# Reordering the products, the background work and the buffer slots of an attention and two-GEMM kernel on one core

## The chip, the cores and the metric

The kernel runs on one NeuronCore of a Trainium2 chip. The metric is device microseconds of one execution, the median of several runs. The profiler names the engines: PE (TensorE, the matmul engine, with its weight loads shown apart as PEld), DVE (VectorE), ACT (ScalarE), POOL (GpSimd) and SP (SyncE, which here only issues DMAs). Each engine works through its own instructions in program order and meets the others at semaphores.

## The reference: what is computed

```python
# q, k, v: (4, 12, 448, 64)
scores = np.where(upper_triangle, -1e9, (q @ k.transpose(0, 1, 3, 2)) / 8)
attn = softmax(scores)
x = (attn @ v).transpose(0, 2, 1, 3).reshape(1792, 768)
h = x @ w_in                                       # w_in (768, 2048)
g = np.maximum(h, 0) + alpha * np.minimum(h, 0)    # alpha (2048,)
out = g @ w_out                                    # w_out (2048, 768)
```

The four inputs q, k, v and alpha and the output are float32; the host hands the two weight matrices over as 64-bit floats.

## The kernel before, in words

**Attention.** 24 pairs of heads are worked through in a software pipeline. The text `ORDER` (line 34) lists the steps of one turn with a lag each: scores (S), row maximum on DVE (MX), exponential on ACT (EX), normalisation on POOL (NO), transposes on PE (PT) and their copies (C), the product with v (AV), and then the split of the resulting piece of x into a rounded high part (XH) and the rest (XL), which goes to DRAM (`lows`, through `store` and `flush`, step ST). Step ED runs background work listed in the table `EARLY` (line 25). "T" there is one pass on POOL over a sum of pieces of x (`t_hi`, `t_lo`), "LD" one load of a raw weight piece.

**Precision.** Every operand of the two GEMMs is a high part plus a low part, so each product takes three matmuls (high by high, high by low, low by high). Weight pieces arrive as raw 64-bit floats (`load_piece`, two buffers `raw`) and are turned into float32 by `start_piece`: an absolute value on ACT (line 147), a clamp on POOL (line 150), four integer passes on DVE (lines 153 to 161), a last addition on POOL (line 164). `split_in` and `split_out` then make the high part on ACT (lines 187, 211) and the low part on POOL (lines 189, 212).

**First GEMM.** The 2048 hidden features are taken in 8 groups g of two chunks, the tokens in two blocks bp of 384 and 512 columns for each of two halves n of the batches; a quad q is one g with one bp (16 quads). A quad gives four outputs: X and Y (chunks 0 and 1 of token half 0), Z and W (the same of token half 1). Quads 0 and 1 (g = 0) are computed plainly (`h_plain`, 12 products each, lines 572 to 578). From quad 2 on a two by two block scheme with seven products is used, plus four products for the last third of the inner dimension (LX, LY, LZ, LW), so 11 steps in the order of `STEPS` (line 516), each of six matmuls (`h_mms`). Partial sums are copied between held PSUM banks on ACT (`h_copy`, lines 580 to 591). `h_act` applies the two-slope function on DVE (lines 603 to 606), `h_split` splits the result g on ACT and POOL (lines 612, 613).

**Second GEMM.** `o_half` (lines 632 to 656) makes one half of a row of output tiles: 128 tokens, 384 columns, six matmuls into one bank, then one addition of that bank to the accumulator `acc` on DVE (line 648; for g = 0 a copy on ACT, line 646). A quad has 12 such halves (bp = 0) or 16 (bp = 1), in the order of `halves_of`: token half, tile, column half. In the loop at lines 930 to 940 the halves of quad q − 1 run two at a time behind the steps 3 and later of quad q. Three PSUM banks serve them; five are held (X, Y, Z, W and V, the product P5).

**What sets the order around the change.** `plan_in` and `plan_out` (lines 702 to 730) place the work on the next weight pieces by step: `begin` is the absolute value and the clamp, `finish` runs all four DVE passes together, issues the next raw load and the last addition; `sub_later` puts a low part off by one step. `background` (line 912) runs this behind the halves of a step. On SP the loads of raw pieces, the stores of the low parts of x, their loads (`load_low`, line 539, four buffers) and the output all stand in one queue, in program order. The pools `wi` (10), `y` (4) and `g` (4) hand out their buffers in turn.

Of the kernel before, what the change touches and what calls it, by code (L numbers as in the profile page):

```python
# [30 lines left out]
}  # L31
LOADV = {0: 2, 1: 2, 2: 2, 3: 1, 9: 4, 10: 3, 11: 2, 12: 2, 13: 2, 14: 1}
TURNS = [(0, 0), (0, 1), (0, 2), (0, 5), (1, 0), (1, 1), (1, 3), (1, 4), (0, 3), (0, 4), (1, 2), (1, 5)]
ORDER = """
NO00+3p NO10+3p MX11+2 NO21+3p NO11+3p EX10+2 EX11+2 MX20+2 NO20+3p MX21+2 EX20+2 NO30+3p MX00+2 EX00+2 AV+4 S2+2 LV+4 PT1+3 PT0+3 PT2+3 EX21+2 MX01+2 EX01+2 C10+3a XH+4 MX30+2 XF+4 XL+4 ED+4 EX30+2 C00+3d C21+3d RC+2 NO01+2p C20+3a LK+0 LQ+0 PT3+3 S0+1 S1+1 SF+1 C30+3a MX10+1 ST+4
"""


@with_exitstack
def kernel(  # L40
# [49 lines left out]
    ident = const.tile([P, P], F32, name="ident")  # L90
# [31 lines left out]
    raws, pieces = {}, {}  # L122

# [13 lines left out]
    def start_piece(kind, f, z):  # L137
# [5 lines left out]
        y = gp["y"].tile([P, NH], F32, tag="y", name=f"y_{kind}{f}_{z}")  # L143
# [29 lines left out]
    def split_in(g, nm):  # L173


        def c(c, z):
            return pieces["i", g * GC + c, z]

        w = slice(0, KW * P)
        t = ws["i", g, nm] = gp["wi"].tile([P, 2, KW * P], F32R, tag="wi", name=f"wi_{g}_{nm}")  # L180
        if nm[0] == "L":
            src = [(slice(z * P, (z + 1) * P), c(int(nm[1]), z)[:, KW * P :]) for z in range(2)]
        else:
            src = [(w, ws["s", nm] if nm in ("S1", "S2", "S4") else c(*{
                "A11": (0, 0), "A12": (0, 1), "A22": (1, 1), "A21": (1, 0), "S3": (1, 0)}[nm])[:, w])]
        for cols, x in src:
            nc.scalar.activation(t[:, 0, cols], x, AF.Copy)
        return lambda: [
            nc.gpsimd.tensor_tensor(out=t[:, 1, cols], in0=x, in1=t[:, 0, cols], op=ALU.subtract)  # L189
            for cols, x in src  # L190
        ]

    def sum_in(g, nm, eng):
# [3 lines left out]
        if nm != "S3":  # L197
            ws["s", nm] = gp["s"].tile([P, KW * P], F32, tag=nm, name=f"{nm}_{g}")
# [6 lines left out]
        else:  # L205
            add_of(ws["s", nm], a(0, 1), ws["s", "S2"], ALU.subtract, eng)

    def split_out(f, z):
# [3 lines left out]
        return lambda: nc.gpsimd.tensor_tensor(out=t[:, 1], in0=y, in1=t[:, 0], op=ALU.subtract)  # L212
# [141 lines left out]
    def transpose_p(p, i):  # L354
        t = T["p", p, i]
        for js in ((0,), (1,)) if i == 2 else (range(t.shape[1]),):
            ps = bank(f"pt_{p}_{i}_{js[0]}")[:, : len(js) * (i + 1) * QP]
            ps = T["pt", p, i, js[0]] = ps.rearrange("p (j c n) -> p j c n", j=len(js), n=QP)
            for j in js:
                for c in range(i + 1):  # L360
                    nc.tensor.transpose(ps[:, j - js[0], c], t[:, j, c * QP : (c + 1) * QP], ident)  # L361
# [60 lines left out]
    def x_hi(p):  # L422
# [3 lines left out]
        else:  # L426
# [14 lines left out]
    def x_lo(p):  # L441
# [8 lines left out]
        (("T3", 0), ("T1", 0), ("T1", 1), ("T3", 1), ("T2", 0), ("T2", 1), ("T4", 0), ("T4", 1))  # L450
# [15 lines left out]
    def run(it, n=None):  # L466
# [4 lines left out]
        "LV": load_v_next, "RC": row_rec, "AV": av, "XH": x_hi, "XF": x_sums, "XL": x_lo, "ST": flush,  # L471
    }
    plan = {}
# [21 lines left out]
    steps["ED"] = lambda p: [fn() for fn in plan.pop(p + 4, ())]  # L495

# [19 lines left out]
    STEPS = ["P1", "P5", "P6", "P2", "P7", "LX", "P3", "LY", "P4", "LZ", "LW"]  # L516
# [29 lines left out]
    def h_bank(q, nm):  # L546
        if (q, nm) not in H:
            H[q, nm] = held[nm] if held else bank(f"h_{q}_{nm}")
# [10 lines left out]
    def h_mms(q, wn, xn, to, first):  # L559
# [3 lines left out]
        for i, (u, k, x) in enumerate(mms):  # L563
# [3 lines left out]
            )  # L567

# [413 lines left out]
```

## Time and profile before

| | us |
|---|---|
| median of 3 runs (lowest, highest) | 710.36 (708.99, 712.32) |
| the profiled execution's own time | 708.73 |
| its span in the trace | 707.0 |
| PE busy in the span | 640.3 (91%) |
| DVE, POOL, ACT busy | 481.3, 380.7, 275.9 |
| mean granted TensorE clock | 0.969 |

Times in the trace count from the start of the span. The busy time of PE is modelled from the starts of its matmuls, so that a matmul that is held up can count as busy; starts are measured. A share of busy time is a mean over stages with different limits, so the stages are read one by one: attention from 0 to 186 us, the plain quads and their second GEMM to 261, quad 2 to 279, the thirteen quads 3 to 15 to 684, and the last sixteen halves after that. A wait is put down to the engine whose semaphore came last.

### The profile page before, as it was taken

The numbers are of one execution on the slowest core, as the hardware profiler recorded it, in microseconds if no ns is written. First come the engines' busy times: TensorE is split into PE (matmuls) and PEld (weight loads), VectorE is DVE, ScalarE is ACT, GpSimd is POOL, SyncE is SP. The second block draws the span as 40 slices with busy tenths as digits, with TensorE's granted clock in tenths as the row PEclk, the third lists the DMA queues.
The fourth block names the chain that finished last, engine by engine and source line by source line (L and its number), as shares of the span: only waits on it lengthen the run. The fifth ranks groups of instructions, "written<-read, shape, count | busy, mean of one in ns | idle before, by whom it ended". The sixth has DMA issues, their size and how long they took to land.

```text
span 707.0 us, 10854 instructions
## 1 busy us (share of the span) xinstructions
PE 640.3 (91%) x3528; PEld 549.1 (78%) x3528; DVE 481.3 (68%) x1114; ACT 275.9 (39%) x763; POOL 380.7 (54%) x536
## 2 busy tenths in 40 slices
PE   7999999999963896999998989998898989889997
PEld 4666666767853795888887978897797889789987
DVE  4788798886446306767667877767786677768464
ACT  5778777876122552332223232222323232231210
POOL 3546676777173605584465367556636664663320
PEclk9999999999987798999999999999999999999999
DMA  5845576545736106854564565447456445645725
GB/s 140 211 116 157 139 186 192 166 125 168 219 115 191 59 26 203 296 166 135 195 212 151 203 201 182 152 171 237 151 201 204 156 163 184 231 131 181 233 80 179
DMA packets 72953, 120.40 MB, mean 170 GB/s; under 512 B 14912, under 2 KB 49472, under 8 KB 72896
## 3 DMA queue, kind: packets, MB, share of 16 engines
q1 hardware_dynamic: 72736, 119.48, 53.3%
q8 instruction: 28, 0.46, 0.3%
q10 hardware_dynamic: 160, 0.23, 0.1%
q14 instruction: 29, 0.24, 0.1%
HBM read 105.00 MB, written 14.68 MB: 169 GB/s over the span
## 4 chain that ended last, share of the span: by engine, by line
PE 53%; DVE 19%; POOL 14%; ACT 4%; DMA 4%; issue 4%; SPq 1%; DVEq 0%; POOLq 0%; ACTq 0%
PE o L643 23%; PE heldY L564 7%; PE a L380 6%; PE s L306 3%; PE pt L361 3%; PE s L298 2%; POOL g_Z L613 2%; POOL y_o L164 2%; PE heldZ L564 2%; PE heldX L564 2%; DVE x_o L153 2%; DVE y_o L157 2%; DVE x_o L161 2%; POOL wi_L L189 2%; POOL wo L212 2%
## 5 line engine op out<-in xcount | busy, mean ns | idle before, releaser
L648 DVE TENSOR_TENSOR acc<-o,acc 128x384 f32<-128x384 f32 x196 | 103.9, 553 | 58.4 <-PE o L643 58.3
L287 POOL TENSOR_SCALAR p<-p,rs 128x128 f32<-128x128 f32 (+3 forms) x164 | 79.0, 504 | 62.9 <-DVE rs L342 54.9
L643 PE MATMUL o<-wo,g_X 128*128 128x384 f32 x336 | 80.3, 347 | 23.7 <-DVE acc L648 21.4
L333 ACT ACTIVATE p<-s,nm 128x256 f32<-128x256 f32 (+3 forms) x168 | 82.0, 496 | 36.1 <-DVE nm L318 35.9
L643 PE MATMUL o<-wo,g_Z 128*128 128x384 f32 x336 | 78.8, 342 | 12.0 <-ACT acc L646 11.0
L643 PEld LDWEIGHTS o<-wo,g_X 128*128 128x128 f32 x336 | 60.5, 192 | 32.4 <-DVE acc L648 27.2
L318 DVE CUSTOM_DVE_ANT_0 s<-s,mask 128x256 f32<-128x256 f32 (+3 forms) x168 | 70.8, 481 | 13.7 <-PE s L298 7.6
L643 PE MATMUL o<-wo,g_Y 128*128 128x384 f32 x336 | 78.1, 340 | 0.3 <-POOL g_Y L613 0.3
L643 PE MATMUL o<-wo,g_W 128*128 128x384 f32 x336 | 77.6, 339 | 0.0
L164 POOL TENSOR_TENSOR y_o<-y_o,x_o 128x384 f32<-128x384 f32 x32 | 32.3, 1008 | 81.2 <-DVE x_o L161 64.3
L643 PEld LDWEIGHTS o<-wo,g_Z 128*128 128x128 f32 x336 | 60.9, 192 | 16.6 <-ACT acc L646 11.8
L164 POOL TENSOR_TENSOR y_i<-y_i,x_i 128x384 f32<-128x384 f32 x32 | 32.4, 1013 | 62.4 <-DVE x_i L161 62.4
L211 ACT ACTIVATE wo<-y_o 128x384 fp32r<-128x384 f32 x32 | 16.8, 525 | 116.0 <-POOL y_o L164 55.6
L643 PEld LDWEIGHTS o<-wo,g_Y 128*128 128x128 f32 x336 | 61.2, 191 | 0.6 <-POOL g_Y L613 0.6
L643 PEld LDWEIGHTS o<-wo,g_W 128*128 128x128 f32 x336 | 61.2, 192 | 0.0
L153 DVE TENSOR_SCALAR x_o<-x_o 128x384 int32<-128x384 int32 x32 | 18.6, 582 | 61.4 <-POOL x_o L150 61.4
L380 PEld LDWEIGHTS a<-ptf,v 128*64 128x64 f32 x384 | 32.7, 136 | 31.2 <-issue 11.9
L613 POOL TENSOR_TENSOR g_Y<-t_Y,g_Y 128x384 fp32r<-128x384 f32 (+1 forms) x16 | 19.7, 1228 | 66.4 <-PE o L643 41.2
L380 PE MATMUL a<-ptf,v 128*64 128x448 f32 (+3 forms) x384 | 51.3, 386 | 2.8 <-DVE ptf L285 2.5
L361 PEld LDWEIGHTS pt<-ident,p 128*128 128x128 f32 x384 | 43.8, 143 | 12.5 <-issue 10.8
L306 PE MATMUL s<-kr,qr 64*128 64x384 f32 (+2 forms) x288 | 46.8, 413 | 3.1 <-ACT p L333 1.9
L361 PE MATMUL pt<-ident,p 128*128 128x128 f32 x384 | 47.6, 277 | 1.9 <-DVE p L349 1.5
(177 smaller groups left out, 1333.7 us busy)
## 6 DMA issues: line engine op xcount, KB each, us to landing
lo_T<-low_T SPq DMA_DIRECT2D x28, 512.0 KB, 5.2
lo_B<-low_B SPq DMA_DIRECT2D x25, 512.0 KB, 4.1
raw_i<-in_moe_w_in_dram SPq DMA_DIRECT2D x32, 384.0 KB, 3.3
raw_o<-in_moe_w_out_dram SPq DMA_DIRECT2D x32, 384.0 KB, 3.2
lo_T<-low_T SPq DMA_DIRECT2D x28, 384.0 KB, 3.5
lo_B<-low_B SPq DMA_DIRECT2D x25, 384.0 KB, 3.6
lo_N<-low_N SPq DMA_DIRECT2D x16, 512.0 KB, 4.4
lo_N<-low_N SPq DMA_DIRECT2D x16, 384.0 KB, 4.2
```

Of the source, the lines that this page charges most:

```text
L153: yield ts(out=x, in0=x, scalar1=3, scalar2=0x3FFFFFF8, op0=ALU.logical_shift_left, op1=ALU.bitwise_and,)
L164: nc.gpsimd.tensor_tensor(out=y, in0=y, in1=xf, op=ALU.add)
L287: eng.tensor_scalar(out=out, in0=x, scalar1=side, scalar2=1.0, op0=ALU.mult, op1=ALU.mult)
L306: nc.tensor.matmul(ps[:, o : o + lim], T["q", p][half(j), i * QP : (i + 1) * QP], T["k", p][half(j), :lim], start=(o == 0), stop=(n > 0 or ...
L318: nc.vector.tensor_tensor_reduce(out=t, in0=t, in1=masks[1] if i == NQ else masks[0][:, (NQ - 1 - i) * QP :], scale=-SCALE, scalar=MOST_F3 ...
L333: nc.scalar.activation(T["p", p, i][:, j, : t.shape[1]], t, AF.Exp, scale=-1.0, bias=T.pop(("nm", p, i, j)), accum_out=T["sm", p][:, z : z ...
L361: nc.tensor.transpose(ps[:, j - js[0], c], t[:, j, c * QP : (c + 1) * QP], ident)
L380: nc.tensor.matmul(out[half(j), c * QP :], vs[b % 2][:, hp, c, j], x[:, c * QP : S], start=(c == 0), stop=(c == NQ),)
L564: nc.tensor.matmul(ps, w[:, u, k * P : (k + 1) * P], x, start=(first and i == 0), stop=(i == len(mms) - 1), skip_group_check=True,)
L613: nc.gpsimd.tensor_tensor(out=l, in0=t, in1=h, op=ALU.subtract)
L643: nc.tensor.matmul(ps[:, :NH], x, w, start=(i == 0), stop=(i == 3 * GC - 1))
L648: nc.vector.tensor_tensor(out=a[:, cols], in0=ps[:, :NH], in1=a[:, cols], op=ALU.add)
```

## The change

- **Order of the products.** `STEPS` puts LY and P4 before P3, so that Y is complete at step 8, not 9.
- **Halves.** For g > 0 `halves_of` goes over the column half first, then token half, then tile. A table `PER` says how many halves follow each step, beginning at step 2; eight of quad 1's halves stay for quad 2. Three banks for the halves become four: V is no longer held and takes one of these in turn.
- **Background work.** `plan_in` and `plan_out` go. Tables `FIRST` (plain quads: lines 1 to 10 behind a product each, 11 to 30 behind a half each), `SECOND`/`CYCLE` and `LATER` (22 steps of two quads) name each operation: abs, clamp, D (a number of DVE passes), add, load, cast and sub (high and low part), S (sums of weight blocks), act, gh, gl (two-slope function, high and low part of g), th and tl (split of a sum of x). Of the D of a step one runs behind each half, the rest at its end; act, gh and gl come ahead of the halves; the rest follows in the order of `KINDS`.
- **Slots.** The buffers of `wi`, `y` (now five) and `g` (now five) are given out first free, first used, and come free when their last use has been issued.
- **Attention.** `EARLY` is rewritten: six of the twelve T of the early part now stand in turn 26, and the first two output pieces' passes move to a table `FRONT`, run at the start of a turn (step E2). The copy of an N piece of x to its high part moves down `ORDER` (XN), the loads of v (LV) behind those of k and q.

```diff
+CYCLE = """
+1: act.1W gl.1Z abs.o2.0 clamp.o2.0
+2: gh.1W gl.1W D.o2.0.2 cast.o1.0 cast.L0.0 abs.o3.0
+3: D.o2.0.2 load cast.S4.0 sub.L0.0 sub.o1.0 clamp.o3.0
+4: D.o3.0.2 add.o2.0 sub.S4.0
+5: D.o3.0.2 load abs.i0.1 clamp.i0.1
+6: D.i0.1.2 add.o3.0
+7: act.2X D.i0.1.1 abs.i1.1 clamp.i1.1
+8: gh.2X gl.2X D.i0.1.1 load D.i1.1.1 cast.o2.0
+9: act.2Y D.i1.1.1 add.i0.1 sub.o2.0 cast.o3.0
+10: gh.2Y gl.2Y D.i1.1.2 load sub.o3.0
+11: act.2Z gh.2Z add.i1.1 abs.i2.1 clamp.i2.1
+"""
...
+FIRST = """
+0: gh.0Y gh.0X gl.0Y gl.0X abs.o2.0 clamp.o2.0
+1: act.0Z cast.o0.0 cast.o1.0 gh.0W gl.0W D.o2.0.1 abs.o3.0
...
+4: D.o2.0.1 D.o3.0.1 load tl th
+5: act.1Y act.1X add.o2.0 D.o3.0.1 tl th
+6: gh.1Y cast.o2.0 D.o3.0.2 load tl
+7: gl.1Y sub.o2.0 add.o3.0
+8: cast.o3.0 abs.i0.1 clamp.i0.1
+9: sub.o3.0 D.i0.1.2
+10: D.i0.1.2 load abs.i1.1 add.i0.1 clamp.i1.1
...
+14: abs.i2.1 clamp.i2.1 S.S1.1
...
+PER = {
+    "q2": [0, 1, 1, 1, 1, 1, 1, 1, 1, 0, 0],
+    "a": [0, 2, 1, 2, 1, 2, 2, 1, 2, 1, 2],
+    "b": [0, 1, 1, 2, 1, 1, 1, 2, 1, 1, 1],
+}
...
-    STEPS = ["P1", "P5", "P6", "P2", "P7", "LX", "P3", "LY", "P4", "LZ", "LW"]
+    STEPS = ["P1", "P5", "P6", "P2", "P7", "LX", "LY", "P4", "P3", "LZ", "LW"]
...
-        if q == 0:
-            return [(n, t, hf) for n in range(2) for hf in range(2) for t in range(nt)]
-        return [(n, t, hf) for n in range(2) for t in range(nt) for hf in range(2)]
+        if quads[q][0] == 0:
+            todo = [(n, t, hf) for n in range(2) for hf in range(2) for t in range(nt)]
+        else:
+            todo = [(n, t, hf) for hf in range(2) for n in range(2) for t in range(nt)]
...
-        for nm in "XYZWV":
+        for nm in "XYZW":
             held[nm] = hold.tile([P, 512], F32, name=f"held{nm}")
-        open_banks(ctx, "psb", 3)
+        open_banks(ctx, "psb", 4)
...
-            for n, st in enumerate(STEPS, 1):
+            per = PER["q2" if q == NBP else "ba"[bp == 0]]
+            for m, st in enumerate(STEPS, 1):
+                n = len(STEPS) * bp + m
                 h_step(q, st)
-                load_low(low_calls.get(n, 0))
+                load_low(low_calls.get(m, 0))
                 h_copy(q, st)
-                if st in ends:
-                    h_act(q, ends[st])
-                for _, i in zip(range(2 if n >= 3 else 0), halves):
+                before(n)
+                ds = micro(n)
+                for _, i in zip(range(per[m - 1]), rest):
                     o_half(q - 1, *i)
-                background(q, n)
+                    run(fn() for _, fn in zip(range(1), ds))
+                behind(n, ds)
```

## Rows read from the trace of the kernel before

**Rows 1.** The page's part 2: PE's busy tenths and granted clock in 40 slices.
```profile
PE   7999999999963896999998989998898989889997
...
PEclk9999999999987798999999999999999999999999
```
**Rows 2.** Busy time by stage: stretch, length, each engine, clock, DMA share, GB/s.
```profile
186.17:212.58 26.41, 20.09 (x89) 15.40 (x89) 13.95 (x24) 5.39 (x12) 14.61 (x17) 0.87 0.49 149
212.58:261.09 48.51, 35.22 (x173) 33.66 (x171) 18.25 (x32) 21.10 (x50) 18.52 (x24) 0.82 0.27 88
261.09:278.68 17.59, 14.69 (x68) 13.65 (x67) 9.13 (x18) 5.71 (x12) 6.90 (x9) 0.81 0.54 179
278.68:684.01 405.33, 376.13 (x1939) 345.43 (x1939) 286.29 (x507) 109.54 (x244) 224.45 (x267) 0.99 0.55 186
684.01:707.00 22.99, 17.40 (x97) 16.42 (x95) 13.20 (x21) 1.26 (x2) 4.03 (x3) 1.00 0.41 138
```
**Rows 3.** Chain that ended last, in order of time: start, length, engine, tile, line, matmuls.
```profile
189.09 1.90 PE a L380 x16
...
420.99 2.08 PE o L643 x12
423.07 1.39 PE heldX L564 x6
```
**Rows 4.** Waits of PE in the whole span: us in total, times, longest.
```profile
PE o L643 <- DVE acc L648: 22.4, 24, 2.2
PE o L643 <- ACT acc L646: 11.0, 1, 11.0
PE h_W L564 <- DMA lo_N<-low_N: 6.3, 1, 6.3
PE heldY L564 <- ACT heldY L591: 4.3, 6, 0.7
```
**Rows 5.** Timeline of SP's queue behind the attention: start, us, issue.
```profile
196.84 0.42 SPq L402 DMA_DIRECT2D low_N<-low_N  x1
...
204.74 0.38 SPq L129 DMA_DIRECT2D raw_i<-in_moe_w_in_dram  x1
205.29 0.36 SPq L544 DMA_DIRECT2D lo_N<-low_N  x1
```
**Rows 6.** DMA issues from 176 to 300 us: count, KB, median us to landing.
```profile
raw_i<-in_moe_w_in_dram SPq DMA_DIRECT2D x8, 384.0 KB, 3.3
...
lo_N<-low_N SPq DMA_DIRECT2D x4, 512.0 KB, 4.4
...
low_N<-low_N SPq DMA_DIRECT2D x2, 224.0 KB, 4.5
```
**Rows 7.** Timeline of ACT in the plain quads, the longest wait.
```profile
224.91 0.55 ACT L147 ACTIVATE x_i<-raw_i 128x384 f32<-128x384 f32 x1 [10.20 <-DMA raw_i<-in_moe_w_in_dram]
```
**Rows 8.** Timeline of DVE in one quad of 512 columns: start, us, instruction, wait.
```profile
477.64 0.36 DVE L153 TENSOR_SCALAR x_i<-x_i 128x384 int32<-128x384 int32 x1 [1.61 <-POOL x_i L150]
...
479.55 1.48 DVE L648 TENSOR_TENSOR acc<-o,acc 128x384 f32<-128x384 f32 x3
```
**Rows 9.** Groups of DVE instructions by shape, 283.3 to 684 us: busy, mean ns.
```profile
L648 DVE TENSOR_TENSOR acc<-o,acc 128x384 f32<-128x384 f32 x180 | 95.1, 553 | 52.1 <-PE o L643 52.1
...
L606 DVE SCALAR_TENSOR_TENSOR t_W<-t_W,m_W 128x512 f32<-128x512 f32 x6 | 9.9, 1656 | 0.2
...
L606 DVE SCALAR_TENSOR_TENSOR t_X<-heldX,t_X 128x512 f32<-128x512 f32 x7 | 4.8, 692 | 0.2
```
**Rows 10.** Busy time of the engines in one period of two quads, columns as in rows 2.
```profile
419.44:481.31 61.87, 57.26 (x302) 52.86 (x301) 45.19 (x80) 17.30 (x39) 35.90 (x44) 1.00 0.55 185
```
**Rows 11.** Timeline of DVE, its last instruction.
```profile
703.05 0.56 DVE L648 TENSOR_TENSOR acc<-o,acc 128x384 f32<-128x384 f32 x1 [0.49 <-PE o L643]
```
**Rows 12.** Waits of PE up to 186.17 us, the longest in total.
```profile
PE a L380 <- DVE ptf L285: 2.5, 5, 0.9
```
**Rows 13.** Groups of POOL instructions, 60 to 186 us, second pass of T.
```profile
L461 POOL TENSOR_TENSOR acc<-acc,xw 128x448 fp32r<-128x448 f32 x11 | 12.7, 1156 | 0.9
```

More of the change, by code (lines that the diff above doesn't have):

```diff
@@ L36 @@
 """
+FIRST = """
+0: gh.0Y gh.0X gl.0Y gl.0X abs.o2.0 clamp.o2.0
+1: act.0Z cast.o0.0 cast.o1.0 gh.0W gl.0W D.o2.0.1 abs.o3.0
+2: gh.0Z gl.0Z sub.o0.0 sub.o1.0 clamp.o3.0 D.o2.0.1 th
+3: D.o2.0.1 tl th
+4: D.o2.0.1 D.o3.0.1 load tl th
[5 more added lines that the diff above has]
+10: D.i0.1.2 load abs.i1.1 add.i0.1 clamp.i1.1
+11: act.1W act.1Z
+12: D.i1.1.2
+13: D.i1.1.2 load add.i1.1
@@ new lines @@
+14: abs.i2.1 clamp.i2.1 S.S1.1
+15: D.i2.1.1 cast.S1.1
+16: D.i2.1.2 sub.S1.1 cast.L1.1
+17: gh.1X D.i2.1.1 load abs.i3.1 add.i2.1 clamp.i3.1 sub.L1.1
+18: gl.1X gh.1W D.i3.1.1 cast.A22.1
+19: gl.1W D.i3.1.2 S.S2.1 sub.A22.1
+20: D.i3.1.1 load S.S3.1 add.i3.1 cast.A11.1
+21: cast.S2.1 sub.A11.1
+22: S.S4.1 cast.S3.1 sub.S2.1
+23: gh.1Z cast.A12.1 sub.S3.1
+24: gl.1Z abs.o0.1 clamp.o0.1 sub.A12.1
+25: D.o0.1.1
+26: D.o0.1.1
+27: D.o0.1.2 load
+28: add.o0.1 abs.o1.1 clamp.o1.1
+29: D.o1.1.1
+30: D.o1.1.1
@@ new lines @@
+"""
+SECOND = """
+1: D.o1.0.1
+2: D.o1.0.1 load cast.o0.0 cast.L0.0
+3: add.o1.0 sub.o0.0 sub.L0.0 cast.S4.0 abs.o2.0 clamp.o2.0
+4: D.o2.0.2 cast.o1.0 sub.S4.0
+5: D.o2.0.2 load sub.o1.0 abs.o3.0 clamp.o3.0
+6: D.o3.0.2 add.o2.0
+7: act.2X D.o3.0.2 load abs.i0.1 clamp.i0.1
+8: gh.2X gl.2X D.i0.1.2 add.o3.0 cast.o2.0
+9: act.2Y D.i0.1.2 load abs.i1.1 clamp.i1.1 sub.o2.0 cast.o3.0
+10: gh.2Y gl.2Y D.i1.1.2 add.i0.1 sub.o3.0
+11: act.2Z gh.2Z D.i1.1.2 load add.i1.1 abs.i2.1 clamp.i2.1
+"""
+CYCLE = """
@@ new lines @@
+1: act.1W gl.1Z abs.o2.0 clamp.o2.0
[9 more added lines that the diff above has]
+11: act.2Z gh.2Z add.i1.1 abs.i2.1 clamp.i2.1
+"""
+LATER = """
+12: act.2W gl.2Z
+13: gh.2W gl.2W D.i2.1.2 S.S1.1 abs.i3.1 clamp.i3.1
@@ L495 @@
     steps["ED"] = lambda p: [fn() for fn in plan.pop(p + 4, ())]
+    steps["E2"] = lambda p: [fn() for fn in front.pop(p + 4, ())]
     order = []
@@ L567, in h_mms @@
             )
+        w_done(g, wn)
+        if xn == "B12":
+            for k in range(KW):
+                w_done("x", bp, k)
     def h_step(q, st):
@@ L644, in o_half @@
                 i += 1
+        g_left[q, n] -= 1
+        if g_left[q, n] == 0:
+            g_free.extend(g_slot.pop((q, BANK[c, n])) for c in range(GC))
         if g == 0:
@@ new lines, in tasks_of @@
+    def tasks_of(text, g, pair):
+        out = {}
+        for line in text.split("\n"):
+            if not line:
+                continue
+            n, todo = line.split(":")
+            for w in todo.split():
+                kind, *arg = w.split(".")
+                if kind == "load":
+                    fn = load_next
+                elif kind == "th":
+                    fn = lambda: t_hi(nc.scalar)
+                elif kind == "tl":
+                    fn = lambda: (t_lo(nc.vector), flush())
+                elif kind in ("act", "gh", "gl"):
+                    q = int(arg[0][0]) + pair
+                    if q < 0 or (q < NBP and pair >= 0 and g):
+                        continue
+                    fn = lambda f={"act": h_act, "gh": g_hi, "gl": g_lo}[kind], q=q, nm=arg[0][1]: f(q, nm)
+                else:
+                    h = g + int(arg[1])
+                    if h >= NG:
+                        continue
+                    if kind == "D":
+                        for _ in range(int(arg[2])):
+                            out.setdefault(int(n), []).append((kind, lambda nm=arg[0], h=h: ops(nm, h, 1)))
+                        continue
+                    if kind == "S":
+                        fn = lambda nm=arg[0], h=h: sum_in(h, nm, nc.vector if h == 1 else nc.gpsimd)
+                    else:
+                        f = {"abs": abs_of, "clamp": clamp, "add": add, "cast": cast, "sub": sub}[kind]
+                        fn = lambda f=f, nm=arg[0], h=h: f(nm, h)
+                out.setdefault(int(n), []).append((kind, fn))
+        for v in out.values():
+            v.sort(key=lambda x: KINDS.index(x[0]))
+        return out
@@ L777, in scores_done @@
         att_a.close()
-        for nm, n in (("t", 4), ("low", 4)):
+        for nm, n in (("t", 3), ("low", 4)):
             gp[nm] = pool("m_" + nm, n, "right")
```

312 lines of the change are left out of this document (146 added, 166 removed), and 10 rows, old and new, of the table EARLY.

## The prediction

> **What bounds the kernel now.** I read the clock and PE in 40 slices first: PE is dense up to slice 11, has a hole in slices 11 to 16 (about 195 to 300 us) where the granted clock also falls, and is dense again with small dents to the end [rows 1]. So the span is PE's work plus what PE loses, and the stages have to be priced one by one. For that I cut the span where the work changes [rows 2] and took PE's own prices from the chain, in places where it runs without waits: two halves 2.08 us, so 1.04 each; a product of 512 columns 1.39; an AV of a pair 1.90 [rows 3]. A product of 384 columns is six matmuls of 384 columns, as a half is: 1.04. Then the loss of a stage is its length less the sum of its pieces:
>
> - 186.17 to 212.58: twelve products of 512 columns and the last AV, 12 x 1.39 + 1.9 = 18.6 us of work in 26.4, loss 7.8.
> - 212.58 to 278.68: 28 halves, three bank-opening matmuls (about 0.7) and eleven products of 384 columns, 29.1 + 0.7 + 11.4 = 41.2 in 66.1, loss 24.9.
> - 278.68 to 684.01: quads 3 to 15, that is 7 x 11 products of 1.39 (107.0), 6 x 11 of 1.04 (68.6) and the halves of quads 2 to 14, 7 x 12 + 6 x 16 = 180 (187.2): 362.8 in 405.3, loss 42.5. One period of two quads takes 61.9 us [rows 10] for 11 x 2.43 + 28 x 1.04 = 55.9, the same rate.
> - the end: sixteen halves, 16.6, in 23.0.
>
> The table of PE's waits names the losses [rows 4]. It shows less than these sums, since a held-up matmul partly counts as busy and since behind a long wait the matmuls run at the lower clock: the granted clock is 0.82 and 0.81 of 2.4 GHz in the two stages behind the two longest waits [rows 2].
>
> **The change part by part.** Attention, 0 to 186 us: the same instructions in other places. The longest entry of PE's waits there is 2.5 us [rows 12], which bounds a gain at about 3. Six T's now stand in one turn of POOL, at least 6 x 1.16 us for their second pass alone [rows 13], and SP's stores of them queue behind; the pair's normalisations that the transposes need come ahead of them. I take 0 and keep 3 on both sides.
>
> The plain products lose 7.8 us through one queue. The last pair's AV ends at 191.0 [rows 3], but its low part is stored only at 196.84, and the load that reads it back goes out at 205.29, behind a load of a raw piece that waited until 204.74 for its buffer [rows 5]; PE waits 6.3 us for it [rows 4] and goes on at the lower clock. After the change that raw load is issued two products later, behind DVE passes in step 4. Two DVE passes of about 0.65 (0.553 for 384 columns [rows 9], scaled to 448) put the store at 192.3; landing takes 4.5 and 4.4 us [rows 6], so the part is there at 201.2. PE wants it when ten products and two thirds of another are done, 186.2 + 1.9 + 10.7 x 1.39 = 203.0. Hidden, with 2 us in hand; if that cover goes, each us late is a us lost. The stage falls to its 18.6.
>
> The halves of quads 0 and 1 wait 11.0 us for one eviction on ACT [rows 4], because ACT stood for 10.2 us at an absolute value whose raw piece had not been loaded [rows 7]. The new tables issue each raw load four steps ahead (step 4 for 8, 6 for 10, 10 for 14), or some 4 to 5.5 us against 3.3 to landing [rows 6], and put act, gh and gl ahead of a step's halves. ACT will still stand now and then, but eight banks are open there and a half fills one in 1.04 us. Eight halves go into quad 2, whose products ran with nothing between them and so outran copies and loads. What is late next is the second output piece: its passes, addition, high and low part need POOL and DVE until about 206 or 207 us by my count, and the fourth half wants it at 204.8 + 3.1 = 207.9. From 186.17 to 278.68 the work is 18.6 + 41.2 = 59.8 in 92.5; I leave 3 us for this edge: a gain of 29.7.
>
> Quads 3 to 15. Of the 22.4 us that halves wait for additions on DVE [rows 4], nearly all fall here. The cause stands in one place: DVE takes up a run of four passes, waits 1.61 us at its head for POOL's clamp, works off the run, and only then, at 479.55, empties three banks in a row [rows 8]. PE had filled all three and stood 2.2 us. After the change the clamp is issued a step before its pass, one pass at a time stands between two additions, and there are four banks. ACT's copies for Y (4.3 us [rows 4]) get one or two halves between P5 and P6 as cover. The runs that stay whole are the two-slope functions of Z and W, three DVE operations each, the last 1.66 us alone [rows 9]; four banks are 4.16 us of halves, so they should mostly fit. The order of the products by itself is worth little: no wait for a part of g is among the large ones [rows 4]; it buys time for the new order of the halves. I let a quarter of the 42.5 stay for what the shorter period uncovers: 10.6, a gain of 31.9. Low end: all of it stays; high end: none.
>
> A rule speaks against packing DVE closer to POOL. The same operation on 512 columns takes 0.692 us when one input comes from PSUM (t_X) and 1.656 when both come from SBUF (t_W) [rows 9], so a large part of DVE's time is already waiting. The Trainium skill ("SBUF — State Buffer", section "Who interferes with whom") says that a DVE instruction with two SBUF inputs, or in a mode that uses both ports, and a GpSimd instruction that reads SBUF block each other, the second until the first is done. The two rows agree with it; by the rule at its hardest the sum would lose the whole gain of these quads (a rival, below).
>
> The end. The order of the halves leaves every output row of the last quad open until its second column half, so seven rows of 384 KB and a half row go out over the last 7.3 us of matmuls, 2.9 MB. The stretch before moved 186 GB/s at a share of 0.55 [rows 2], so about 340 at most, 8.5 us: an estimated 1.2 us more behind the last addition, which now ends 3.4 us before the span does [rows 11]. Against that the first eight halves no longer stand behind DVE, save about 1.2 us for W. Of 6.4 lost I count 0.5 gained.
>
> **Sum.** 707.0 − 29.7 − 31.9 − 0.5 = 644.9 us of span. The profiled run's own time is 1.7 above its span and the median of the runs 1.6 above that: 648.
>
> **The rivals.** (a) DVE's queue stays the limit of quads 3 to 15 and half of the loss stays: 10.6 more, 659. For it: DVE is busy 45.2 of 61.9 us in a period [rows 10], which is 81% of 55.9. Against it: in most of a period it waits for PE (52.1 us before additions alone, over the stage [rows 9]). (b) The plain stage stays held by ACT standing at raw pieces; half of the 32.7 lost there stays instead of 3: 13 more, 661. For it: still two raw buffers, and each load waits for the passes of an earlier piece. Both (a) and (b): 672.
>
> (c) Blocking by POOL makes DVE the bound. If the two masking passes of each of a period's eight pieces were also held up by 1.656 − 0.692 = 0.96 us, DVE would need 45.2 + 16 x 0.96 = 60.6 us for a period, more than PE's 55.9, and the gain in quads 3 to 15 is gone: 680. This is the page's rule at work on every piece; the trace shows it for t_W.
>
> (d) Slower. In each quad four absolute values stand on ACT ahead of the copies X to Y, V, Y to Z and Y to W, which the next products read. A raw load is issued two or three steps ahead, about 5 to 6 us for 3.3 to landing. If SP reaches it late, because it stands behind a load that waits for PE, ACT holds the copies and PE stands. Over 52 such places (13 quads) it takes 62 / 52 = 1.2 us each to eat the gain; at 1.4 us each the time is 720. It decides once loads land some 4 us later than I count. Against it: SP's waits for buffers end with PE's steps, which lie behind it by then.
>
> (e) The change doesn't do what it says: buffers given out by last use put new waits into the casts, as large as those removed, and the time stays at 710.
>
> **How the numbers follow.** What a measurement of this kernel can tell from no change is 0.5%, 3.5 us, about what the three runs spread. Likeliest, 648, alone: 633 to 658 (down: neither remainder of 3 and 10.6 us, and a little from attention; up: the second remainder doubled). Chances: likeliest 0.58, (a) 0.15, (b) 0.12, both 0.06, (c) 0.03, (d) 0.04, (e) 0.02. Faster takes all but (d) and (e): 0.94. The range goes from the likeliest's low end to past both (a) and (b), 633 to 674.
>
> **What would show it.** Right: the first half of quad 0 starts near 205 us and quad 3 near 248; the clock stays at 1.00 from 186 us on; a period of two quads takes 57 to 58 us; the waits for DVE's additions fall from 22.4 us to under 8; the end behind the last product takes 22 to 23. Wrong: a wait of several us for `lo_N` or for ACT's eviction again (b); periods of 59 and more with waits for additions (a), with DVE near all busy and its masking passes over 1 us (c); waits of products for copies on ACT that stand behind raw loads (d).

## The result and the profile after

The changed kernel takes 649.0 us (median of 4 runs, 647.32 to 651.08) against 710.25 us for the kernel before, measured beside it (median of 4, 708.99 to 712.32): a ratio of 0.9136, 95% interval 0.91 to 0.9173. The prediction said 648, 633 to 674. Its total is right; two of its terms are not, in opposite directions, and most of this part is about them.

The profiled execution took 649.86 us with a span of 648.1. The page's part 2, answering to [rows 1]:

```profile
PE   7889998999995899799999999999999999999996
...
PEclk9998999999998889899999999999999999999999
```

The hole in the middle is narrower and the dents behind it are gone. Busy time by stage, columns as in [rows 2]; the cuts are the same points of the program: attention with the first products, twelve plain products of 512 columns, 28 halves, quad 2, quads 3 to 15, the last sixteen halves.

```profile
0.00:181.23 181.23, 169.31 (x1169) 115.87 (x1170) 143.85 (x522) 134.68 (x445) 117.00 (x222) 0.99 0.60 163
181.23:201.09 19.86, 18.78 (x89) 14.42 (x89) 8.79 (x15) 5.15 (x11) 9.26 (x11) 1.00 0.75 238
201.09:236.22 35.13, 27.04 (x124) 25.50 (x123) 23.92 (x38) 16.52 (x40) 21.41 (x25) 0.81 0.38 122
236.22:256.00 19.78, 19.78 (x115) 19.77 (x114) 13.18 (x22) 9.57 (x22) 12.19 (x15) 1.00 0.73 231
256.00:625.10 369.10, 365.23 (x1939) 344.11 (x1939) 298.42 (x501) 108.18 (x243) 235.02 (x263) 1.00 0.62 199
625.10:648.10 23.00, 17.11 (x97) 16.47 (x96) 11.76 (x21) 1.26 (x2) 2.59 (x2) 0.97 0.46 158
```

Against [rows 2], with the prediction's terms beside them:

| stage | before | after | change | predicted |
|---|---|---|---|---|
| attention, to quad 1's first product of 512 columns | 186.17 | 181.23 | −4.9 | 0 |
| plain products, halves of quads 0 and 1, quad 2 | 92.51 | 74.77 | −17.7 | −29.7 |
| quads 3 to 15 | 405.33 | 369.10 | −36.2 | −31.9 |
| end | 22.99 | 23.00 | 0.0 | −0.5 |
| span | 707.0 | 648.1 | −58.9 | −62.1 |

PE's longest waits, answering to [rows 4] (engine and line, what it waited for: us in total, times, longest):

```profile
PE o L774 <- POOL wo L322: 4.7, 1, 4.7
PE a L493 <- DMA v<-in_v_dram: 4.6, 4, 3.0
PE heldY L681 <- ACT heldY L712: 3.7, 1, 3.7
PE o L774 <- POOL g_X L740: 2.5, 1, 2.5
...
PE h_W L681 <- DMA lo_N<-low_N: 1.1, 1, 1.1
```

The 22.4 us of halves waiting for DVE's additions and the 11.0 us for ACT's eviction have no entry any more. What is left are single waits, nearly all in the first 265 us. A period of two quads, columns as above (both ends are the start of the same product):

```profile
401.56:457.44 55.88, 55.88 (x301) 53.00 (x301) 48.15 (x82) 17.14 (x39) 38.38 (x44) 1.00 0.66 205
```

That is PE's floor of 55.9 us as the prediction worked it out; before, a period took 61.87 [rows 10].

**Where the middle lost 12 us.** It begins on SP, at the end of the attention (start, us, issue):

```profile
184.60 0.38 SPq L515 DMA_DIRECT2D low_N<-low_N  x1
185.07 5.22 SPq L515 DMA_DIRECT2D low_T<-acc  x8
190.48 0.33 SPq L229 DMA_DIRECT2D raw_o<-in_moe_w_out_dram  x1
190.90 0.57 SPq L515 DMA_DIRECT2D low_N<-low_N  x1
195.50 0.32 SPq L661 DMA_DIRECT2D lo_N<-low_N  x1
```

The eight stores of turn 26's six T's (four of 224 KB, two of 192, two of 32) hold SP for 5.22 us: the issues themselves take 0.32 to 0.77 us each, 3.6 in all, and the rest lies between them, 0.92 of it in one gap before the seventh. Behind them stand the load of the raw output piece and the store of the last low part of x. ACT stands at the raw piece's absolute value, and the high part of g Z, which needs nothing from it, stands behind that (in brackets: idle time before, and what ended it):

```profile
194.93 0.55 ACT L245 ACTIVATE x_o<-raw_o 128x384 f32<-128x384 f32 x1 [5.88 <-DMA raw_o<-in_moe_w_out_dram]
...
257.38 0.54 ACT L245 ACTIVATE x_i<-raw_i 128x384 f32<-128x384 f32 x1 [2.76 <-DMA raw_i<-in_moe_w_in_dram]
```

The raw piece is the last of the four output pieces of g = 0, o3 in `FIRST`; o2 and o3 make the second column half, which this text and the prediction call the second output piece. So POOL, in program order too, starts late on everything that these need:

```profile
196.80 1.02 POOL L740 TENSOR_TENSOR g_Z<-t_Z,g_Z 128x384 fp32r<-128x384 f32 x1 [6.66 <-ACT g_Z L736]
197.77 2.67 POOL L322 TENSOR_TENSOR wo<-y_o,wo 128x384 fp32r<-128x384 f32 x2
200.42 0.50 POOL L248 TENSOR_SCALAR x_o<-x_o 128x384 f32<-128x384 f32 x1
...
207.94 1.31 POOL L262 TENSOR_TENSOR y_o<-y_o,x_o 128x384 f32<-128x384 f32 x1 [1.89 <-DVE x_o L259]
209.21 0.99 POOL L322 TENSOR_TENSOR wo<-y_o,wo 128x384 fp32r<-128x384 f32 x1
```

PE's waits from here to quad 3, without those under 1 us:

```profile
199.14 0.72 PE L681 MATMUL h_W<-lo_N,wi_L 128*128 128x512 f32 x2 [1.08 <-DMA lo_N<-low_N]
...
210.26 1.01 PE L774 MATMUL o<-wo,g_X 128*128 128x384 f32 x2 [4.65 <-POOL wo L322]
...
225.85 0.44 PE L774 MATMUL o<-wo,g_X 128*128 128x384 f32 x1 [2.54 <-POOL g_X L740]
...
264.14 1.73 PE L681 MATMUL heldY<-xw,wi_S 128*128 128x512 f32 x4 [3.73 <-ACT heldY L712]
```

The first comes from the late store, the second from the late output pieces: what PE waits for there is the low part of o2, which stands on POOL behind o3's addition (207.94 and 209.21, above), since `KINDS` puts a step's additions ahead of its low parts and line 7 of `FIRST` has both. The third is not theirs: it stays, at 3.1 and 2.5 us, in the two kernels below in which the stores are moved. Behind the second wait PE runs at a granted clock of 0.50 from 210.26 to 216.34 us, behind the third at 0.67 from 225.85 to 231.00; over the twenty halves of this stage the clock is 0.81, and they take 35.1 us where 21.5 (20 x 1.04 and the three bank-opening matmuls) would do. The last wait is another place: in quad 3 ACT stood 2.76 us at a raw piece (257.38, above), DVE stood 2.21 us for that piece's clamp, ACT stood 3.89 us for DVE at the high part of g Z, and the copy of X to Y, behind all this, came late.

### The profile page after: what moved, and what is told of

It is laid out like the page before. It is cut to its first block, busy times and chain, and to the rows that moved or that the text cites. A ratio compares the mean times of both kernels' runs of the same rounds, so it can differ in the third digit from the quotient of the medians.

```text
span 648.1 us, 10850 instructions
## 1 busy us (share of the span) xinstructions
PE 617.3 (95%) x3528; PEld 536.1 (83%) x3528; DVE 499.9 (77%) x1114; ACT 275.4 (42%) x763; POOL 397.5 (61%) x536
## 4 chain that ended last, share of the span: by engine, by line
PE 76%; DVE 6%; DMA 5%; SPq 4%; issue 3%; POOL 3%; ACT 2%; POOLq 0%; DVEq 0%; ACTq 0%
PE o L774 31%; PE heldY L681 10%; PE heldX L681 7%; PE a L493 5%; PE heldZ L681 5%; PE pt L474 4%; PE s L419 4%; PE s L411 3%; DMA v<-in_v_dram 2%; PE heldW L681 2%; PE h_V L681 2%; SPq L354 2%; DMA raw_i<-in_moe_w_in_dram 1%; SPq L357 1%; DMA qr<-in_q_dram 1%
## 5 line engine op out<-in xcount | busy, mean ns | idle before, releaser
L782 DVE TENSOR_TENSOR acc<-o,acc 128x384 f32<-128x384 f32 x196 | 107.4, 551 | 67.5 <-PE o L774 67.2
L400 POOL TENSOR_SCALAR p<-p,rs 128x128 f32<-128x128 f32 (+3 forms) x164 | 80.7, 515 | 56.5 <-DVE rs L455 45.1
L446 ACT ACTIVATE p<-s,nm 128x256 f32<-128x256 f32 (+3 forms) x168 | 82.4, 497 | 23.5 <-DVE nm L431 22.4
L774 PE MATMUL o<-wo,g_Z 128*128 128x384 f32 x336 | 76.6, 335 | 0.0
L774 PEld LDWEIGHTS o<-wo,g_X 128*128 128x128 f32 x336 | 62.5, 194 | 12.1 <-POOL wo L322 4.9
L493 PEld LDWEIGHTS a<-ptf,v 128*64 128x64 f32 x384 | 26.7, 136 | 36.8 <-issue 13.4
L493 PE MATMUL a<-ptf,v 128*64 128x320 f32 (+3 forms) x384 | 48.5, 387 | 5.4 <-DMA v<-in_v_dram 4.6
L474 PE MATMUL pt<-ident,p 128*128 128x128 f32 x384 | 48.2, 278 | 2.4 <-DVE p L462 1.5
L396 ACT ACTIVATE ptf<-pt 128x512 f32<-128x512 f32 (+1 forms) x72 | 38.5, 578 | 14.5 <-PE pt L474 14.5
L419 PE MATMUL s<-kr,qr 64*128 64x128 f32 (+2 forms) x288 | 41.4, 397 | 2.5 <-ACT ptf L396 1.0
L248 POOL TENSOR_SCALAR x_i<-x_i 128x384 f32<-128x384 f32 x32 | 18.1, 565 | 39.2 <-ACT x_i L245 38.9
L736 ACT ACTIVATE g_Z<-t_Z 128x384 fp32r<-128x384 f32 (+1 forms) x16 | 9.2, 577 | 74.8 <-DVE t_Z L727 74.8
```

Source lines behind the costliest of these rows:

```text
L396: eng.activation(out, x, AF.Copy, scale=side)
L400: eng.tensor_scalar(out=out, in0=x, scalar1=side, scalar2=1.0, op0=ALU.mult, op1=ALU.mult)
L419: nc.tensor.matmul(ps[:, o : o + lim], T["q", p][half(j), i * QP : (i + 1) * QP], T["k", p][half(j), :lim], start=(o == 0), stop=(n > 0 or ...
L446: nc.scalar.activation(T["p", p, i][:, j, : t.shape[1]], t, AF.Exp, scale=-1.0, bias=T.pop(("nm", p, i, j)), accum_out=T["sm", p][:, z : z ...
L493: nc.tensor.matmul(out[half(j), c * QP :], vs[b % 2][:, hp, c, j], x[:, c * QP : S], start=(c == 0), stop=(c == NQ),)
L774: nc.tensor.matmul(ps[:, :NH], x, w, start=(i == 0), stop=(i == 3 * GC - 1))
```

## The experiments

Each kernel ran beside the kernel before on the same chip; ratios are to that. The kernel before had medians of 709.46, 708.82 and 708.77 us in the three sets.

### The attention: one step of its order

Working on the first question, why the attention became shorter, showed an error in the text above the prediction. It says that the copy of an N piece of x moves down. In the diff it is the other way round: the N piece's copy on DVE (XN) stays where XH stood, behind C10, and the copy of the B pieces on ACT (XH) moves up, ahead of EX21, MX01, EX01 and C10. Two kernels test this, one each way: the changed kernel with XH moved back, and the kernel before with XH alone moved up (XN, which is new there, stays behind C10). The diffs show the part of `ORDER`. The first:

```diff
-PT2+3 XH+4 EX21+2 MX01+2 EX01+2 C10+3a XN+4 MX30+2
+PT2+3 EX21+2 MX01+2 EX01+2 C10+3a XH+4 XN+4 MX30+2
```

> The changed kernel with one step of the attention's order put back: the high part of B pieces on ACT stands again behind the copy C10, not ahead of EX21. Theory: this step alone made the attention shorter, since DVE's sums and low part wait for it and the pair's period hangs on them. Then the first 512-column product of quad 1, at 181.2 us in the changed kernel, starts at 187 to 190, and the span is 6 to 9 us longer. Rival: the background work moved out of the middle turns (T passes, first output pieces) made the attention shorter. Then it stays within 1.5 us of 181.2 and the time within 2 us.

Measured: 658.12 us (657.59 to 660.08), ratio 0.9288, 0.9264 to 0.9312. Quad 1's first product of 512 columns starts at 189.76 us instead of 181.23. The second:

```diff
-PT2+3 EX21+2 MX01+2 EX01+2 C10+3a XH+4 MX30+2
+PT2+3 XH+4 EX21+2 MX01+2 EX01+2 C10+3a XN+4 MX30+2
```

> The kernel before with that one step alone moved up. Theory: the attention ends 6 to 9 us earlier (186.2 us to 177 to 180) and the whole is as much shorter, 701 to 704. Rival: no change in the attention, 710.

Measured: 700.11 us (699.17 to 700.41), ratio 0.9873, 0.9847 to 0.9899. That product starts at 176.56 instead of 186.17. So this step is worth 8.5 to 9.6 us, both ways, and 9.1 and 9.4 by the medians. Where it sits is seen on DVE, in its groups over the first 200 us (busy, mean ns | idle just before, what ended it). The kernel before:

```profile
L437 DVE TENSOR_TENSOR acc<-a,acc 128x448 f32<-128x448 f32 x16 | 9.6, 622 | 13.5 <-ACT xw L283 9.2 <-ACT xb L283 4.3
```

The same with XH up (the line numbers shift by 3):

```profile
L440 DVE TENSOR_TENSOR acc<-a,acc 128x448 f32<-128x448 f32 x16 | 9.6, 619 | 0.9 <-ACT xw L283 0.9
```

DVE's additions of x stood 13.5 us for ACT's copies, which stood behind exponentials that they don't need; the row maxima queued behind the additions. In the changed kernel this idle time is 0.1 us, and with XH back it is 12.8. PE's table never showed this as one wait: it was spread over the whole pipeline.

The changed kernel gains only 4.9 of these 9 to 10 us. Its 4.6 us of waiting for v suggested the moved load LV:

```diff
-S2+2 PT1+3
+S2+2 LV+4 PT1+3
...
-LQ+0 LV+4 PT3+3
+LQ+0 PT3+3
```

> The changed kernel with the loads of v put back to their old place in a turn, ahead of the transposes and the loads of q and k. Theory: PE's waits for v (4.6 us in four places, the longest 3.0, with a lower clock behind it between 40 and 60 us) go away, quad 1's first product starts at 177 to 178.5 us, the time falls by 3 to 4 us. Rival: the loads of q and k, now later, take over the wait, and the time stays within 1 us.

Measured: 649.75 us (648.38 to 650.42), ratio 0.9163, 0.9141 to 0.9185: no change. Its waits:

```profile
PE s L419 <- DMA qr<-in_q_dram: 3.4, 1, 3.4
...
PE a L493 <- DMA v<-in_v_dram: 1.1, 2, 0.7
```

Most of the wait for v goes, and one for q comes, of about the same size. What the attention still gives back is not the place of this one load.

The size of that gain is itself uncertain. Five kernels below leave the changed kernel's attention as it is (those with three banks, bunched passes, both, both with halves in twos, and the old steps). In their traces quad 1's first product of 512 columns starts between 182.48 and 184.89 us, so 181.23 is the earliest of six and the gain against 186.17 lies between 1.3 and 4.9 us. A difference of a us or two between two traces of this attention shows nothing.

### The end of the attention: the stores of the T's

The stores of the six T's of turn 26 are kept back and issued three products later; the T's on POOL stay where they are.

```diff
+    def t_early():
+        kept, stores[:] = stores[:], []
+        t_hi(nc.gpsimd)
+        t_lo(nc.gpsimd)
+        late_stores.extend(stores)
+        stores[:] = kept
...
-                        fns.append(lambda: (t_hi(nc.gpsimd), t_lo(nc.gpsimd)))
+                        fns.append(t_early if n == 26 else lambda: (t_hi(nc.gpsimd), t_lo(nc.gpsimd)))
...
+            if n == 3:
+                stores.extend(late_stores)
+                flush()
             started(n)
```

> The changed kernel with the stores of the six T passes of turn 26 issued three products later, behind the store and the read-back of the last low part. Theory: those eight stores (5.2 us of SP's queue) hold the load of the fourth output piece until 190.5 us, ACT stands at its absolute value until 194.9, and with it the low parts of g and of the first pieces; without them the load goes out before 186, PE's waits for that piece (4.65 and 0.78 us), for the read-back (1.1) and the lower clock behind them go, and the time falls by 5 to 8 us. Rival: POOL's and DVE's own order sets when that piece is ready; the wait stays within 1 us of 4.65 and the time within 1.5 us.

Measured: 644.04 us (642.22 to 647.99), ratio 0.9092, 0.9056 to 0.9129; the kernel with LV back, of the same set, has 0.9141 to 0.9185. SP's queue in it:

```profile
184.98 0.37 SPq L229 DMA_DIRECT2D raw_o<-in_moe_w_out_dram  x1
187.29 0.32 SPq L515 DMA_DIRECT2D low_N<-low_N  x1
190.26 0.32 SPq L663 DMA_DIRECT2D lo_N<-low_N  x1
190.67 4.60 SPq L515 DMA_DIRECT2D low_T<-acc  x9
```

and PE's waits, where that for lo_N has no entry any more:

```profile
PE o L776 <- POOL wo L322: 2.6, 2, 2.0
PE heldY L683 <- ACT heldY L714: 2.1, 1, 2.1
```

So the median falls by 5 us, the low end of what was expected, but the stores explain less of the middle than that: from quad 1's first product of 512 columns to quad 3 it takes 70.9 us instead of 74.8, a gain of 3.9 of the 12 us. The wait for the second output piece halves (4.7 to 2.6) and does not go; what keeps the rest, POOL's and DVE's own order by the trace, was not tried alone. The other 3.6 us of this trace lie in quad 3, which takes 30.1 us instead of 33.8, with a wait of heldY of 2.1. They are not shown to come from the stores: the kernel with the old steps, below, has the same 30.2 and 2.1 with the stores in place, and the next kernel has 33.5 and 3.7 with the stores moved.

The same with LV at its old place and the raw loads of the attention at their old turns, 3 and 4, so that three suspects go at once:

```diff
-            after(6, "LQ", load_next)
+            after(3, "LQ", load_next)
```

> The changed kernel with the late stores of the T passes (5 us faster when tried alone), the loads of v at their old place and the first two raw loads in their old turns 3 and 4. Theory: what the attention still lost against the kernel before with only the one step moved up (181.2 against 176.6 us for quad 1's first product) is these loads' places; then that product starts at 177 to 178 and the time is 639 to 641. Rival: it is the T passes or the output pieces of the last turns; then it starts at 180 or later and the time is 643 to 645.

Measured: 644.2 us (641.32 to 645.16, 5 runs), ratio 0.9077, 0.9052 to 0.9103, the same as without the two loads; the products start at 180.37, PE waits 3.7 us for q. The middle takes 70.6 us, a gain of 4.2, so the stores are worth about 4 of the 12 us. What keeps the changed kernel's attention some 4 us above the 176.6 of the kernel before with XH up stays open; part of it is seen in PE's waits for v and q together, 4.6 us here and 2.2 there. These two kernels, at 644 us, are the fastest found.

### Quads 3 to 15: what took the waits for additions away

The changed kernel gives the halves a fourth bank, spreads them, splits runs of DVE passes and reorders the products, all at once. First the fourth bank alone, in the kernel before:

```diff
-            H[q, nm] = held[nm] if held else bank(f"h_{q}_{nm}")
+            H[q, nm] = held[nm] if nm in held else bank(f"h_{q}_{nm}")
...
-        for nm in "XYZWV":
+        for nm in "XYZW":
...
-        open_banks(ctx, "psb", 3)
+        open_banks(ctx, "psb", 4)
```

> The kernel before with V taken from the banks of the halves, so that four serve them instead of three; nothing else. Theory: its runs of four passes behind a wait for the clamp hold DVE some 3.5 us, which three banks (3.1 us) don't cover and four (4.2 us) mostly do; the waits for the additions fall from 22.4 us to under 10 and the time by 12 to 25 us. Rival: V takes the fourth bank back when it is wanted, or the runs are longer than four banks; under 4 us.

Measured: 680.81 us (679.13 to 681.59), ratio 0.96, 0.9579 to 0.9621. One bank gives 28 us, more than expected. The waits for additions fall from 22.4 us [rows 4] to 1.4 us, and the others stand:

```profile
PE o L643 <- ACT acc L646: 10.2, 1, 10.2
PE h_W L564 <- DMA lo_N<-low_N: 6.4, 1, 6.4
PE heldY L564 <- ACT heldY L591: 4.3, 6, 0.7
```

The gain is larger than the 22.4 us that the table listed, as the prediction's sums by stage had it (42.5 lost, less shown): a matmul that is held up counts partly as busy. Then the fourth bank taken away from the changed kernel (the line of `open_banks` alone, 4 to 3):

> The changed kernel with three PSUM banks for the halves and V instead of four. Theory: the fourth bank is what lets PE run on while DVE works through a run that stays whole (the two-slope functions, 2 to 3 us each, four of them in a period of two quads); with three banks (3.1 us of halves, one of them lent to V) PE waits about 1 to 3 us in each period, and the time grows by 7 to 20 us. Rival: placing the passes one by one between the additions is enough; the time grows by less than 3 us.

Measured: 649.12 us (648.14 to 651.3), ratio 0.9161, 0.9137 to 0.9184: nothing. PE waits once, 0.5 us, for an addition. Quads 4 to 14 take 28.08 us (384 columns) and 27.81 (512) each, to the hundredth what they take in the changed kernel. The next one, with four banks, runs all of a step's DVE passes behind all of its halves again:

```diff
                     o_half(q - 1, *i)
-                    run(fn() for _, fn in zip(range(1), ds))
```

> The changed kernel with all DVE passes of a step behind its halves, instead of one behind each half. Theory: the tables place at most three passes in a step, the clamps come a step ahead, and four banks cover a run of 1 to 2 us; the time grows by 0 to 4 us. Rival: the interleaving itself removed the waits for the additions; they come back, 2 us or more in each period, and the time grows by 15 us or more.

Measured: 650.13 us (649.05 to 652.16), ratio 0.917, 0.9142 to 0.9199: at most a microsecond or two. Both of these edits together:

> The changed kernel with three banks and with all passes of a step behind its halves, both together; each alone cost nothing. Theory: the fourth bank and the passes laid one by one between the additions are two remedies for one wait, each enough by itself; with both gone it comes back, since a run of two or three passes and a two-slope function behind it are longer than three banks: 8 to 25 us longer than the changed kernel, as waits for the additions on DVE. Rival: what did it was the clamp placed a step ahead, so that DVE doesn't stand at a run's head; then it is within 4 us of 649.

Measured: 650.54 us (646.81 to 653.69), ratio 0.9174, 0.9138 to 0.9209. Still nothing, and the quads again take 28.08 and 27.81 us, so that theory fell: neither bank nor interleaving is needed once the rest is there. Then halves two at a time from the third step on, as before, on top of both:

```diff
-    "a": [0, 2, 1, 2, 1, 2, 2, 1, 2, 1, 2],
-    "b": [0, 1, 1, 2, 1, 1, 1, 2, 1, 1, 1],
+    "a": [0, 0, 2, 2, 2, 2, 2, 2, 2, 2, 0],
+    "b": [0, 0, 2, 2, 2, 2, 2, 2, 0, 0, 0],
```

> As the run with three banks and bunched passes, and the halves again two behind each step from the third on, as before the change. Theory (the spread of the halves matters too): a further 5 us or more of waits for the additions. Rival: the spread matters little; within 3 us of the run without it.

Measured: 689.38 us (684.7 to 691.25), ratio 0.9713, 0.9677 to 0.9749: 39 us lost, but not where it was looked for:

```profile
PE heldY L681 <- ACT heldY L712: 28.4, 12, 4.7
...
PE o L774 <- DVE acc L782: 1.2, 1, 1.2
```

The halves hardly wait for additions even so. P6 waits for ACT's copy of X to Y, once in nearly every quad. One such place, in order of time:

```profile
421.89 0.63 ACT L736 ACTIVATE g_Z<-t_Z 128x512 fp32r<-128x512 f32 x1 [4.27 <-DVE t_Z L727]
422.42 0.47 ACT L712 ACTIVATE heldY<-heldX 128x384 f32<-128x384 f32 x1
...
422.95 1.10 PE L681 MATMUL heldY<-xw,wi_S 128*128 128x384 f32 x4 [2.96 <-ACT heldY L712]
```

ACT waits 4.27 us for DVE at the high part of g Z, the copy stands behind it, and without halves between P5 and P6 PE has nothing else to do. So the halves behind the second step are the cover of that copy. The kernel before had no halves there either and lost only 4.3 us at this copy [rows 4]. A likely reason, not tried alone, is that the new tables put the two-slope function of Z and its high part into one step, the last before the copy, where the kernel before had them in steps 10 and 11. That the additions hardly waited here, with three banks, no interleaving and halves in twos, points to the tables' split of a piece's four passes into two and two, with the clamp a step earlier; that split was not undone by itself, and PE's waits at heldY gave DVE time as well.

The order of the products and the steps of the low loads, put back in the changed kernel:

```diff
-["P1", "P5", "P6", "P2", "P7", "LX", "LY", "P4", "P3", "LZ", "LW"]
+["P1", "P5", "P6", "P2", "P7", "LX", "P3", "LY", "P4", "LZ", "LW"]
```

> The changed kernel with the old order of the products (P3 ahead of LY and P4, so that Y is complete a step later) and the loads of the low parts of x as before to match. Theory: by itself the order is worth little, since no half waited for Y before the change either; within 2 us. Rival: g of Y comes too late for the new order of the halves or holds ACT and POOL at its place in the table; 5 us or more longer.

Measured: 649.94 us (648.05 to 651.99), ratio 0.9168, 0.9141 to 0.9196: nothing.

Last, the two small edits of the kernel before together, XH up and the fourth bank:

> The kernel before with two small edits, the high part of B pieces moved up in the attention and the fourth bank. Theory: the two act in different stages and add, 9 and 28 us: 671 to 674, and what the rest of the change is worth is the remaining 22 to 25 us. Rival: they overlap (an earlier attention brings transfers of the next stage closer): 677 or more.

Measured: 670.11 us (669.0 to 672.25), ratio 0.9455, 0.943 to 0.948. They add up: 9.4 + 28.0 = 37.4, measured 38.7. Two edits of a few lines give some 39 of the change's 61 us. Against this kernel's trace the changed kernel's is 16.0 us shorter from quad 1's first product of 512 columns to quad 3 (74.8 against 90.8), 1.5 to 1.6 shorter in each of the quads of 384 columns from quad 4 on (28.08 against 29.6), and 4.5 longer in the attention. Of the waits left in it,

```profile
PE o L646 <- ACT acc L649: 9.4, 1, 9.4
PE h_W L567 <- DMA lo_N<-low_N: 6.4, 1, 6.4
PE heldX L567 <- DMA lo_B<-low_B: 4.4, 1, 4.4
PE heldY L567 <- ACT heldY L594: 4.3, 6, 0.7
```

the first two belong to the plain stages, which only the new tables touch.

## Why the prediction was right, and where it was not

**Attention (0 predicted, with 3 on both sides; −4.9 measured, −1.3 to −4.9 over six traces of the same attention).** Two steps failed. XH was read the wrong way round in the diff, so the one move that mattered was not costed. And "the longest entry of PE's waits there is 2.5 us, which bounds a gain at about 3" is no bound: XH moved alone gained 9.6 us, with no wait of PE longer than that to point to. The price of the queue showed in the waits of the engine that stood (DVE, 13.5 us), and PE merely got its work later. The move is worth 8.5 us inside the changed kernel, and other moves, not settled, give part of it back, so that the 0 is off by no more only because a gain and losses, none of them costed, offset each other in part.

**Plain products, halves and quad 2 (−29.7 predicted, −17.7 measured).** The step that failed is "I leave 3 us for this edge"; the loss left is 74.8 − 59.8 = 15.0 us. The edge was named rightly, the second output piece. It was put at 206 or 207 us, 1 to 2 us behind the first half; the low part that PE waited for was done at 210.2, 9.1 us behind the first half at 201.09. The six T's stores on SP were named, in the attention's part, as queueing, and then left out of the sum of the next stage, where the raw load and the store of the last low part stood behind them for 5.2 us. The store went out 9.7 us behind quad 1's first product of 512 columns instead of the 6.1 worked out (192.3 − 186.2), which used up the 2 us in hand: PE waited 1.1 us. The stores are worth about 4 of the 12 us missed (74.8 to 70.9 and 70.6). The rest, some 8 us, stays open as far as experiments go: in both of those kernels it lies in the twenty halves, which still take 32.6 and 32.4 us for 21.5, with waits for POOL and a clock of 0.84; POOL's and DVE's order in these steps was seen in the trace and not tried alone. The sum had no term at all for the lower clock behind a wait of this stage.

**Quads 3 to 15 (−31.9 predicted, −36.2 measured).** The cause was read rightly: runs of four passes at a late clamp against three banks. The remainder of 10.6 us was mis-sized. It is 369.1 − 362.8 = 6.3, and nearly all of it is quad 3, 33.8 us against 27.8 for every later quad of 512 columns: its one wait of 3.73 us and the lower clock behind it. A period is at its floor of 55.9, not at 57 to 58. The prediction gave no share to each part, and the runs show why none can be given: the fourth bank alone takes 28 us off the kernel before, and nothing is lost without it in the changed one. Bank and tables are two cures of one wait; which line of the tables is the cure was not tried. That the order of the products is worth little by itself held.

**The end (−0.5 predicted, 0.0 measured).** The bunched output is there, and a little dearer than the estimated 1.2 us: the last addition,

```profile
642.53 0.56 DVE L782 TENSOR_TENSOR acc<-o,acc 128x384 f32<-128x384 f32 x1 [0.49 <-PE o L774]
```

ends 5.0 us before the span does, 1.6 more than before [rows 11].

**The sum.** The span came out 3.2 us over the 644.9 predicted (−4.9, +12.0, −4.3, +0.5, rounded). The median lies 0.9 above the profiled span, not 3.3, which hides that. So 648 against 649.0 is nearer than the terms were: the main cause was read rightly, but the closeness is luck.

**The rivals.** (a) fell: no half of quads 3 to 15 waits for an addition. (b) came true in size: it left half of the 32.7 us of the plain stages and quad 2, and 15 stayed. ACT did stand at a raw piece, 5.88 us with SP's stores as the cause (0.76 with the stores moved), and at later raw pieces of the stage for other reasons (3.40 us at 213.21). The total did not move only because the other terms gave 9 us more. (c) fell as a bound, though some passes of DVE did become longer. DVE's groups by shape in quads 3 to 15 (mean ns behind the busy time), before:

```profile
L157 DVE SCALAR_TENSOR_TENSOR y_o<-raw_o,x_o 128x384 int32<-128x384 int32 x24 | 13.4, 559 | 2.2
...
L605 DVE TENSOR_SCALAR m_W<-t_W,alpha_sb 128x512 f32<-128x512 f32 x6 | 2.9, 487 | 0.2
```

and after:

```profile
L255 DVE SCALAR_TENSOR_TENSOR y_o<-raw_o,x_o 128x384 int32<-128x384 int32 x24 | 22.2, 924 | 0.5
...
L726 DVE TENSOR_SCALAR m_W<-t_W,alpha_sb 128x512 f32<-128x512 f32 x6 | 7.8, 1302 | 0.2
...
L727 DVE SCALAR_TENSOR_TENSOR t_W<-t_W,m_W 128x512 f32<-128x512 f32 x6 | 5.2, 874 | 0.2
```

The masking pass of line 157 (255 after the change) takes 0.92 instead of 0.56 us for an output piece and 0.78 for an input piece, m_W 1.30 instead of 0.49, while t_W falls from 1.66 [rows 9] to 0.87. The stretching moved from one operation to another. DVE is busy 48.2 us of a period instead of 45.2 [rows 10], where the rival needed 60.6. The Trainium skill ("SBUF — State Buffer", section "Who interferes with whom") says that the order of issue, not the shape of the operation, decides who blocks; these rows agree as far as they go: the same operations on the same shapes take other times in another order, but they don't show which engine issued first. (d) happened at one place of 52, quad 3, by way of DVE, and in the kernel with halves in twos its near kin cost 28.4 us of waits: ACT standing in front of the copy X to Y is the weak point of the new tables, and the halves behind the second step cover it. (e) fell.

**What would show it.** Right: waits for additions under 8 (none), the end at 22 to 23. Better than said: the period. The first half of quad 0 started at 201.1, not 205, thanks to the attention alone. Wrong: quad 3 at 256, not 248, and the clock, which was 1.00 to 201 us and then 0.81 for 35 us.

## What to carry to other kernels

Before costing a move in an engine's order, list what the moved instruction waits for and what stands behind it, on DMA queues too: eight stores put at the end of a stage delayed one load of the next stage by 5 us. In a software pipeline read the idle time of every engine by what ended it, not the matmul engine's waits alone. Where engine B empties banks that engine A fills, try one more bank before rewriting a schedule, and test each part of a change alone in the old kernel and missing in the new one: the difference tells which parts are two cures of one wait. A median that falls is not yet a gain in the stage that was changed: read the stages of both traces.

## What was not expected of the hardware

A wait cost more than its length. With the fourth bank 21 us of listed waits went (22.4 to 1.4) and 28 us of time, which may be the list alone, since a held-up matmul can count as busy. Elsewhere it was the clock: quad 3 takes 6.0 us more than the later quads of its shape for a wait of 3.73 us, and in the kernel with the T's stores moved 2.3 us more for a wait of 2.07, at a granted clock of 1.00. The 3.73 us stand in a stretch of 6 us whose granted clock is 0.72, with 1.00 again in the 10 us behind it:

```profile
264.00:270.00 6.00, 5.86 (x21) 5.07 (x22) 5.21 (x8) 3.33 (x9) 5.03 (x7) 0.72 0.89 315
270.00:280.00 10.00, 10.00 (x52) 9.04 (x51) 6.61 (x12) 1.88 (x5) 8.38 (x11) 1.00 0.74 213
```

And a row of stores is not free for the queue that issues it: eight held SP for 5.22 us, of which the issues themselves were 3.6, and nine for 4.60 us, with 3.8 of issues, in the kernel that moved them.
